# Smaller load pieces, a copy on another engine, and one hand-written list of steps between attention and experts

## Chip, cores and metric

One core of one Trainium2 chip. The metric is the device time of the kernel in microseconds (us). The engines are named as the profile names them: PE (matmul), PEld (its weight load), DVE (VectorE), ACT (ScalarE), POOL (GpSimd) and SP, which here only issues transfers.

## What is computed

Attention of 8 batches and 8 heads over 576 positions, in two forms that are added, and then an expert layer on the result (8 experts, 4608 tokens, one expert per token):

```python
q_d = q.reshape(B, H, Sd, factor, D).mean(axis=3)      # factor 4, Sd 144, k_d and v_d alike
out_up = np.repeat(sm_attn(q_d, k_d, v_d), factor, axis=2)
mask = np.abs(pos[:, None] - pos[None, :]) < factor     # local form: 7 neighbours
scores = np.where(mask, scale * np.matmul(q, k.transpose(0, 1, 3, 2)), -1000000000.0)
attn = np.exp(scores - np.max(scores, axis=-1, keepdims=True))
out_local = np.matmul(attn / (np.sum(attn, -1, keepdims=True) + 1e-09), v)
x = (out_up + out_local)                                # as 4608 rows of 512
...
logits = x @ w_gate
expert_idx = np.argmax(logits, axis=1)
gate_w = probs[np.arange(N), expert_idx]                # softmax of the logits
h = np.maximum(x_sorted[lo:hi] @ w1[e], 0.0)            # tokens of expert e
y_sorted[lo:hi] = h @ w2[e]                             # F = 1024
return gate_w[:, None] * y
```

## The kernel before, in words

The attention part is a software pipeline of 32 passes, one for each pair of heads. A table `PASS` lists pairs of a step and a lag; `steps(i)` walks it and calls each step for pass `i - lag`. The order of the table is the order in which each engine gets its instructions. Steps that the text speaks of:

- `load_qk` (L119) and `load_vd` (L207) load a pair's queries and keys (tile qk, one row per partition, queries then keys) and the values that are to be pooled (tile vd, 72 partitions); `load_vw` (L211) loads the local form's values. All are issued by SP, and each waits there until its buffer is free.
- `pool_qk` (L219, L225; tiles qkt, qkd) and `pool_v` (L230, L236; tiles vdt, vds) sum four neighbours on POOL in two steps each.
- `s_loc` (L245 adds the mask, L251 the scores; bank pS) on PE, then on DVE the maximum mx (L264), a subtraction (L268), after the exponential on ACT (L271) the sums (L274), the reciprocals and the scaling (L290); PE turns the result (L329). `s_d` (L305) has the pooled form's scores, `max_d` (L310, L313) their maximum. `add_up` (L385) adds both forms into the tile XT.
- Routing of a batch's rows (`r_mm` to `r_ix`, once per 4 or 5 tiles of 128 tokens) gives each token a row number. `x_rows` (L523, L525) turns a tile's tokens and evicts them into a row buffer xr, and `scatter` (L549, L550) writes them to the expert's rows in device memory (xs) by an indirect transfer, issued by POOL.

The expert part reads rows back with `x_load` (L586, issued by SP), turns them on DVE and splits them in two parts (`prep`: L617, ACT L621, DVE L622), multiplies by W1 (`s1`: L674 to L676, evicted by ACT L678 and DVE L679) and by W2 (`s2`: L688 to L690). The first 256 rows of expert 0 (`EARLY`) are read and multiplied before the last batch is routed, as those rows are surely full by then; `prep(0, 0, 1)` and the eight `s1(0, f, EARLY)` stand between the last passes. Rows 256 to 511 are read once the last scatter is done.

Where the passes end, the program before issues whole groups: `steps(31)`, then the first `x_load`, then `steps(32)`, the routing of the last batch's first four tiles, and so on (the end of the function below). Warm-up matmuls on zeros (`warm`, L138) stand ahead of pass 0 and behind passes 0, 1 and 2. The running count of tokens per expert, crun, gets its start value by a copy on DVE behind pass 2 (L925).

Of the kernel before, what the change touches and what calls it, by code (L numbers as in the profile page):

```python
# [29 lines left out]
KPAD = (NG - 1) * QB + KW  # L30
R = 4
# [12 lines left out]
WARM = (9, 5, 8, 5)  # L44
# [46 lines left out]
def attention_moe_kernel(ctx: ExitStack, tc: tile.TileContext, qk, vw, vd, wg, w1, w2, cst, csb, out):  # L91
# [33 lines left out]
    nc.scalar.dma_start(maskb, csb[:, B_MASK:])  # L125
# [9 lines left out]
    def warm(n, late=False):  # L135
        p = bank() if late else wp
        for _ in range(n):
            nc.tensor.matmul(p, wsrc[:, :128], wsrc, start=True, stop=True)  # L138
# [100 lines left out]
    def s_loc(i):  # L239
# [8 lines left out]
        for c in range(NC):  # L248
            for h, t in ((0, 0), (1, 1), (0, 1), (1, 0)):
# [3 lines left out]
                                 x[r, QPAD + g * QB:QPAD + g * QB + KW],  # L253
# [142 lines left out]
    def r_mm(m, tiles):  # L396
        c = tiles[0] * 128
        p = RS[m, "p"] = bank()
# [10 lines left out]
    def r_lg(m, tiles):  # L409
        lg = RS[m, "lg"] = rp.tile([128, 384], F32, name="over", bufs=1)  # L410
        w = 256 if len(tiles) == 4 else 384
        nc.scalar.activation(lg[:, :w], RS[m, "p"][:, :w], AF.Copy)

    def r_turn(m, tiles):
        lg = RS[m, "lg"]
        p = RS[m, "p"] = bank()
# [6 lines left out]
    def r_max(m, tiles):  # L423
        T = len(tiles)
        RS[m, "pl"] = RS[m, "p"][:, :T * 32].rearrange("p (t e) -> p t e", e=32)[:, :, :E]
        RS[m, "m"] = rp.tile([128, 5], F32, name="rm")
        nc.vector.tensor_reduce(RS[m, "m"][:, :T], RS[m, "pl"], axis=AX.X, op=OP.max)

    def r_sub(m, tiles):
        T = len(tiles)  # L430
        d = RS[m, "d"] = RS[m, "p"][:, 256:296].rearrange("p (t e) -> p t e", e=E)
        nc.vector.tensor_sub(d[:, :T], RS[m, "pl"], RS[m, "m"][:, :T, None].to_broadcast([128, T, E]))

    def r_exp(m, tiles):
        T = len(tiles)
        ex = RS[m, "ex"] = rp.tile([128, 5, E], F32, name="re")
        nc.scalar.activation(ex[:, :T], RS[m, "d"][:, :T], AF.Exp)

    def r_top(m, tiles):
        T = len(tiles)  # L440
        sc = RS[m, "sc"] = RS[m, "p"][:, 320:360].rearrange("p (t e) -> p t e", e=E)
# [632 lines left out]
```

## Time and profile before

| | us |
|---|---|
| three runs, median (lowest to highest) | 647.17 (645.33 to 647.36) |
| the profiled execution, its own time | 644.67 |
| its span in the profile | 642.9 |
| PE busy, share of the span | 96% |
| DVE, ACT, POOL busy | 55%, 53%, 35% |

The profile is of one execution. Times in rows count from the start of its span, and 1.8 us of the execution lie around that. The attention passes fill about the first 175 us, the passage into the experts ends near 225 us, and the experts take the rest.

### The profile page before, as it was taken

The numbers are of one execution on the slowest core, as the hardware profiler recorded it, in microseconds if no ns is written. First come the engines' busy times: TensorE is split into PE (matmuls) and PEld (weight loads), VectorE is DVE, ScalarE is ACT, GpSimd is POOL, SyncE is SP. The second block draws the span as 40 slices with busy tenths as digits, with TensorE's granted clock in tenths as the row PEclk, the third lists the DMA queues.
The fourth block names the chain that finished last, engine by engine and source line by source line (L and its number), as shares of the span: only waits on it lengthen the run. The fifth ranks groups of instructions, "written<-read, shape, count | busy, mean of one in ns | idle before, by whom it ended". The sixth has DMA issues, their size and how long they took to land.

```text
span 642.9 us, 15721 instructions
## 1 busy us (share of the span) xinstructions
PE 617.6 (96%) x6123; PEld 507.9 (79%) x6123; DVE 352.3 (55%) x691; ACT 343.3 (53%) x941; POOL 226.6 (35%) x348
## 2 busy tenths in 40 slices
PE   7899999999979899999999999999999999999994
PEld 4678887787768798888888888888888888888873
DVE  5999988888854573751571174175038166115020
ACT  4899999999964353543452263264235154223120
POOL 7877899999924311111111101101011111110111
PEclk9999999999989999999999999999999999999997
DMA  8998999999862794383274276258137537010001
GB/s 286 286 269 285 292 302 286 292 280 290 239 195 84 187 304 136 122 224 90 84 191 138 66 187 192 68 155 213 56 109 183 181 112 197 35 47 1 34 18 43
DMA packets 68612, 108.65 MB, mean 169 GB/s; under 512 B 15724, under 2 KB 39804, under 8 KB 68496
## 3 DMA queue, kind: packets, MB, share of 16 engines
q1 hardware_dynamic: 62080, 87.78, 49.0%
q0 software_dynamic: 5984, 19.01, 7.9%
q8 instruction: 66, 1.08, 0.8%
q14 instruction: 50, 0.41, 0.2%
q10 hardware_dynamic: 432, 0.37, 0.2%
HBM read 87.09 MB, written 23.67 MB: 172 GB/s over the span
## 4 chain that ended last, share of the span: by engine, by line
PE 68%; issue 10%; POOL 7%; DMA 5%; DVE 5%; ACT 2%; SPq 1%; POOLq 0%; another core or an unknown queue 0%; DVEq 0%; ACTq 0%
PE p L675 8%; PE p L674 8%; PE p L676 8%; PE p L690 7%; PE p L688 7%; PE p L689 7%; POOL xs L550 2%; DMA vd<-in_vd_dram 2%; PE pD L305 2%; POOL vdt L230 2%; PE pX L770 2%; PE pX L789 2%; PE pX L342 1%; PE pS L251 1%; PE pX L329 1%
## 5 line engine op out<-in xcount | busy, mean ns | idle before, releaser
L695 POOL DMA_INDIRECT out_dram<-y,tix x39 | 37.9, 971 | 213.3 <-ACT y L707 201.9
L674 PE MATMUL p<-xh,w1h 128*128 128x512 f32 (+1 forms) x288 | 106.4, 370 | 0.8 <-ACT xh L621 0.7
L675 PE MATMUL p<-xl,w1h 128*128 128x512 f32 (+1 forms) x288 | 105.7, 367 | 0.8 <-DVE xl L622 0.8
L676 PE MATMUL p<-xh,w1l 128*128 128x512 f32 (+1 forms) x288 | 105.5, 366 | 0.0
L688 PE MATMUL p<-w2h,hh 128*128 128x512 f32 x256 | 101.1, 395 | 0.0
L689 PE MATMUL p<-w2l,hh 128*128 128x512 f32 x256 | 99.8, 390 | 0.5 <-DVE w2l L664 0.5
L690 PE MATMUL p<-w2h,hl 128*128 128x512 f32 x256 | 99.9, 390 | 0.0
L679 DVE SCALAR_TENSOR_TENSOR hl<-p,hh 128x512 fp32r<-128x512 f32 (+1 forms) x72 | 45.5, 632 | 94.3 <-ACT hh L678 93.6
L678 ACT ACTIVATE hh<-p 128x512 fp32r<-128x512 f32 (+1 forms) x72 | 39.6, 551 | 78.1 <-PE p L676 75.6
L707 ACT ACTIVATE y<-p,gi 128x512 f32<-128x512 f32 x32 | 22.0, 689 | 91.2 <-PE p L690 86.8
L674 PEld LDWEIGHTS p<-xh,w1h 128*128 128x128 f32 x288 | 54.7, 190 | 10.7 <-ACT xh L621 1.1
L675 PEld LDWEIGHTS p<-xl,w1h 128*128 128x128 f32 x288 | 54.7, 190 | 9.6 <-DVE xl L622 0.9
L676 PEld LDWEIGHTS p<-xh,w1l 128*128 128x128 f32 x288 | 54.6, 190 | 8.7
L689 PEld LDWEIGHTS p<-w2l,hh 128*128 128x128 f32 x256 | 48.1, 188 | 10.6 <-DVE w2l L664 0.9
L690 PEld LDWEIGHTS p<-w2h,hl 128*128 128x128 f32 x256 | 48.1, 188 | 10.2
L688 PEld LDWEIGHTS p<-w2h,hh 128*128 128x128 f32 x256 | 48.1, 188 | 9.5
L664 DVE TENSOR_TENSOR w2l<-raw,w2h 128x512 fp32r<-128x512 f32 x64 | 43.3, 681 | 2.1 <-DMA xs<-xr,ix 1.5
L622 DVE TENSOR_TENSOR xl<-pX,xh 128x512 fp32r<-128x512 f32 x38 | 24.7, 684 | 35.2 <-ACT xh L621 34.2
L194 ACT ACTIVATE w1h<-raw 128x512 fp32r<-128x512 f32 (+1 forms) x72 | 42.1, 584 | 0.0
L550 POOL DMA_INDIRECT xs<-xr,ix x36 | 36.4, 1012 | 15.6 <-ACT xr L525 6.9
L663 ACT ACTIVATE w2h<-raw 128x512 fp32r<-128x512 f32 x64 | 39.8, 626 | 2.8 <-DMA xs<-xr,ix 2.8
L230 POOL TENSOR_TENSOR vdt<-vd 72x512 f32<-72x512 f32 x32 | 40.9, 1279 | 0.3
(152 smaller groups left out, 1240.1 us busy)
## 6 DMA issues: line engine op xcount, KB each, us to landing
raw<-in_w_dram SPq DMA_DIRECT2D x59, 512.0 KB
qk<-in_qk_dram SPq DMA_DIRECT2D x32, 583.0 KB
vw<-in_vw_dram SPq DMA_DIRECT2D x32, 320.0 KB
vd<-in_vd_dram SPq DMA_DIRECT2D x32, 288.0 KB
xrow<-xs SPq DMA_DIRECT2D x32, 192.0 KB
xrow<-xs SPq DMA_DIRECT2D x32, 128.0 KB
xs<-zs SPq DMA_DIRECT2D x6, 512.0 KB
raw<-in_w_dram SPq DMA_DIRECT2D x20, 128.0 KB
```

What stands on the lines that cost most here:

```text
L194: nc.scalar.activation(hi[:, s], src[:, s], AF.Copy)
L230: nc.gpsimd.tensor_add(t2, v[:, 0:2], v[:, 2:4])
L550: ins = nc.gpsimd.indirect_dma_start(out=xs, out_offset=bass.IndirectOffsetOnAxis(ap=IDX[m, t], axis=0), in_=xr, in_offset=None)
L663: nc.scalar.activation(hi, src, AF.Copy)
L664: nc.vector.tensor_sub(lo, src, hi)
L674: nc.tensor.matmul(p, wh[:, fs], xh[:, k, r], start=(k == 0), stop=False)
L675: nc.tensor.matmul(p, wh[:, fs], xl[:, k, r], start=False, stop=False)
L676: nc.tensor.matmul(p, wl[:, fs], xh[:, k, r], start=False, stop=(k == 3))
L679: nc.vector.scalar_tensor_tensor(hl[:, f, r], p, 0.0, hh[:, f, r], op0=OP.max, op1=OP.subtract)
L688: nc.tensor.matmul(p, hh, wh, start=(f == 0), stop=False)
L689: nc.tensor.matmul(p, hh, wl, start=False, stop=False)
L690: nc.tensor.matmul(p, hl, wh, start=False, stop=(f == 7))
```

## The change

It has six parts.

1. The tile qk gets two halves of 586 elements, each with a pad of 2 (the queries' half is filled up to the keys' length), and its load writes the halves as two pieces per partition. The tile vd gets four rows of 256 with a pad of 2, and its load four pieces per partition. The reads on POOL and PE use the new strides.
2. The mask is loaded by SP, between the first two loads of qk; before, by ACT.
3. The copy into crun runs on ACT.
4. The warm-up: 4 matmuls behind pass 0; in passes 2 and 3 a step `keep`, right behind `s_loc`, with 7 and 5.
5. `early_count` comes one pass sooner.
6. The last pass, what is left of the others, the last batch's routing and the early part of expert 0 become one list of single steps, `TAIL`. Steps that were one function (turn and evict rows; matmul, evict and subtract of an expert block; the two halves of a split weight) are single entries of it.

```diff
+KOFF = KPAD + 2
-WARM = (9, 5, 8, 5)
+WARM = (9, 4, 7, 5)
...
-        QK[i] = p1.tile([128, QPAD + KPAD], F32, name="qk", bufs=3)
-        nc.sync.dma_start(QK[i], qk[i])
+        QK[i] = p1.tile([128, 2 * KOFF], F32, name="qk", bufs=3)
+        nc.sync.dma_start(QK[i].rearrange("p (a x) -> p a x", a=2)[:, :, :KPAD], qk[i].rearrange("p (a x) -> p a x", a=2))
...
-    nc.scalar.dma_start(maskb, csb[:, B_MASK:])
+    nc.sync.dma_start(maskb, csb[:, B_MASK:])
...
-        VD[i] = p1.tile([DC, R, 2, 2, D], F32, name="vd")
-        nc.sync.dma_start(VD[i].rearrange("p r c h d -> p (r c h d)"), vd[i])
+        VD[i] = p1.tile([DC, R, 4 * D + 2], F32, name="vd")
+        nc.sync.dma_start(VD[i][:, :, :4 * D], vd[i].rearrange("p (r x) -> p r x", r=R))
...
-            return bass.AP(tensor=x.tensor, offset=x.offset + r, ap=[x.ap[0], [QPAD + HALO, 2], [R, SD], [2, 2]])
+            return bass.AP(tensor=x.tensor, offset=x.offset + r, ap=[x.ap[0], [KOFF + HALO, 2], [R, SD], [2, 2]])
...
-        v = VD[i]
+        v = VD[i][:, :, :4 * D].rearrange("p r (c h d) -> p r c h d", c=2, h=2)
...
+    def keep(i):
+        if 2 <= i < len(WARM):
+            warm(WARM[i])
+
     PASS = (
-        (exp_loc, 1), (rb_turn, 5), (t_d0, 3), (rc_place, 6), (eps, 2), (max_d, 1), (inv, 2), (s_loc, 0),
+        (exp_loc, 1), (rb_turn, 5), (t_d0, 3), (rc_place, 6), (eps, 2), (max_d, 1), (inv, 2), (s_loc, 0), (keep, 0),
...
+    TAIL = (
+        (exp_loc, 30), (s_loc, 31), (max_d, 30), (pool_v2, 30), (r_mm, 3, FIRST4), (eps, 29), (inv_d, 29),
...
+        (r_lg, 3, FIRST4), (sums, 30), (scatter, 2, 6), (e_d0, 28), (s_d, 31), (sub_loc, 31), (pool_v, 31),
+        (pool_v2, 31), (r_turn, 3, FIRST4), (r_max, 3, FIRST4), (x_tr, 2, 7), (x_ev, 2, 8), (norm_d, 29),
+        (r_sub, 3, FIRST4), (eps, 30), (scatter, 2, 8), (x_ev, 2, 7), (shut,), (t_d1, 29), (x_in,), (max_d, 31),
...
+        (r_cs, 3, FIRST4), (x_tr, 3, 1), (ld_vw, 30), (s1_mm, 7), (sums, 31), (x_ev, 3, 3), (r_eps, 3, FIRST4),
+        (ld_vw, 31), (add_up, 29), (eps, 31), (s1_mm, 4), (t_d1, 30), (x_ev, 3, 2), (s1_hi, 7), (x_ev, 3, 1),
...
+        (out_d, 30), (s1_lo, 7), (t_d0, 31), (e_d0, 31), (w2_in,), (t_d1, 31), (e_d1, 31), (r_last, 3, FIRST4),
+        (w2_hi, 0), (s1_mm, 5), (s1_hi, 4), (add_up, 30), (pv_d, 31), (pv_loc, 31), (scatter, 2, 7), (w2_hi, 1),
+        (out_d, 31), (w2_hi, 3), (w2_hi, 2), (scatter, 3, 3), (s1_lo, 4), (add_up, 31), (scatter, 3, 2), (w2_lo, 1),
...
+        (r_run, 3, LAST5), (w2_lo, 5), (scatter, 3, 6), (scatter, 3, 5), (totals,), (s1_lo, 2), (s1_mm, 0),
+        (s1_hi, 0), (s1_mm, 1), (s1_hi, 1), (scatter, 3, 8), (s1_lo, 0), (scatter, 3, 4), (scatter, 3, 7), (s1_lo, 1),
+    )
...
-    for i in range(NP):
+    for i in range(NP - 1):
         steps(i)
-        if i + 1 < len(WARM):
-            warm(WARM[i + 1], i >= 3)
+        if i == 0:
+            warm(WARM[1])
         if i == 2:
-            nc.vector.tensor_copy(crun, cf[:, C_CAP:C_CAP + E])
+            nc.scalar.copy(crun, cf[:, C_CAP:C_CAP + E])
...
-    steps(NP)
-    route_b(m, first)
...
-    totals()
+    for f, *a in TAIL:
+        f(*a)
```

`x_in` of the list is the first `x_load`, with the tiles that its rows are split into.

On DVE the copy into crun stood behind the sums of pass 2 and ahead of the pooled form's maximum. This is the place in the difference of DVE's instructions:

```order
 L268 TENSOR_TENSOR A<-pS,mx 128x2x5x64
 L274 TENSOR_REDUCE smd<-A 128x10
-L925 COPY crun<-cf 128x8
 L310 TENSOR_REDUCE mxd<-pD 128x3
 L282 RECIPROCAL pD<-smd 128x10
```

It is gone from there. The same place in the difference of ACT's instructions, where A is the scores' tile and AT the turned one:

```order
 L336 ACTIVATE AT<-pX 128x232
 L336 ACTIVATE AT<-pX 128x348
+L1032 COPY crun<-cf 128x8
 L271 ACTIVATE A<-A 128x640
 L277 ACTIVATE smd<-smd 128x13
```

The copy now stands ahead of the next pass's exponential.

POOL at the last pass, before: the scatter of tile 6 of batch 2, the last pair's value sums, the scatters of tiles 7 and 8, and the row numbers read back for expert 0:

```order
L550 DMA xs_83<-xr_126,ix_4003 42112x514
L230 TENSOR_TENSOR vdt_4296<-vd_4082 72x512
L236 TENSOR_TENSOR vds_4370<-vdt_4296 72x256
L549 MEMSET spacer_116 1x1
L550 DMA xs_83<-xr_126,ix_4003 42112x514
L549 MEMSET spacer_116 1x1
L550 DMA xs_83<-xr_126,ix_4003 42112x514
L605 CAST tix_4524<-gi_4318 128x2
```

And now:

```order
L557 DMA xs_83<-xr_126,ix_4004 42112x514
L230 TENSOR_TENSOR vdt_4247<-vd_4080 72x512
L236 TENSOR_TENSOR vds_4249<-vdt_4247 72x256
L556 MEMSET spacer_116 1x1
L557 DMA xs_83<-xr_126,ix_4004 42112x514
L482 TENSOR_TENSOR crun_112<-crun_112,cs_4430 128x8
L497 CAST ix_4521<-pos_4519 128x4
L556 MEMSET spacer_116 1x1
L557 DMA xs_83<-xr_126,ix_4004 42112x514
```

The second scatter is now that of tile 8, and the third, that of tile 7, stands behind the count and the row numbers of the last batch's first four tiles. In the program the first `x_load` stood behind the first of these scatters and now stands behind the second.

SP at the same place, before: value loads of the last pairs (vw), the read-back of expert 0's first rows (xrow0) and its gates (gi), three loads of raw W2, and the last pair's values:

```order
L211 DMA vw_4271<-in_vw_dram 128x640
L586 DMA xrow0_4313<-xs_83 32x8x128 x4
L598 DMA gi_4318<-xs_83 128x2x2
L168 DMA raw_4320<-in_w2_dram 128x2x512
L168 DMA raw_4322<-in_w2_dram 128x2x512
L168 DMA raw_4324<-in_w2_dram 128x2x512
L211 DMA vw_4388<-in_vw_dram 128x640
```

And now:

```order
L593 DMA xrow0_4282<-xs_83 32x8x128 x4
L605 DMA gi_4383<-xs_83 128x2x2
L211 DMA vw_4437<-in_vw_dram 128x640
L211 DMA vw_4455<-in_vw_dram 128x640
L168 DMA raw_4536<-in_w2_dram 128x2x512
L168 DMA raw_4538<-in_w2_dram 128x2x512
L168 DMA raw_4540<-in_w2_dram 128x2x512
```

Both value loads now stand behind the read-back and ahead of the W2 loads.

## Rows read from the trace of the kernel before

**Rows 1.** The page: busy us, share of the span, instructions, by engine.
```profile
PE 617.6 (96%) x6123; PEld 507.9 (79%) x6123; DVE 352.3 (55%) x691; ACT 343.3 (53%) x941; POOL 226.6 (35%) x348
```

**Rows 2.** Windows: stretch, its length, busy us by engine, clock, DMA share, GB/s.
```profile
20.00:40.00 20.00, 18.42 (x472) 14.85 (x476) 19.45 (x38) 18.78 (x72) 15.19 (x18) 1.00 0.97 282
...
80.00:100.00 20.00, 19.78 (x488) 16.45 (x487) 17.46 (x44) 19.36 (x74) 19.24 (x27) 1.00 1.00 296
...
120.00:140.00 20.00, 19.40 (x481) 16.05 (x483) 16.26 (x38) 19.06 (x69) 19.24 (x26) 1.00 0.95 294
...
180.00:200.00 20.00, 15.71 (x200) 12.79 (x198) 9.35 (x30) 10.12 (x33) 3.76 (x10) 0.91 0.50 146
...
240.00:630.00 390.00, 389.57 (x1748) 321.86 (x1747) 163.06 (x263) 150.16 (x271) 49.46 (x95) 1.00 0.42 118
```

**Rows 3.** Timeline of the start: start, us, instruction, [idle before and its releaser].
```profile
5.72 0.33 PE L245 MATMUL pS<-mask,cb 64*64 64x320 bf16 x4 [0.95 <-DMA mask<-in_csb_dram]
...
14.09 0.76 PE L329 MATMUL pX<-cf,A 128*128 128x128 f32 x5
...
14.23 0.82 DVE L264 TENSOR_REDUCE mx<-pS 128x10 f32<-128x640 f32 x1 [0.44 <-PE pS L251]
...
16.53 1.26 POOL L230 TENSOR_TENSOR vdt<-vd 72x512 f32<-72x512 f32 x1
16.56 2.37 DVE L925 COPY crun<-cf 128x8 f32<-128x8 f32 x1
...
17.75 1.14 POOL L219 TENSOR_TENSOR qkt<-qk 128x576 f32<-128x576 f32 x1
...
18.84 0.59 DVE L310 TENSOR_REDUCE mxd<-pD 128x3 f32<-128x432 f32 x1
```

**Rows 4.** The chain that ended last, at the tail: start, us, what.
```profile
174.98 3.51 DMA xs<-xr,ix
...
183.97 0.74 DVE p L617
...
212.00 3.29 DMA xs<-xr,ix
...
222.08 1.91 DVE pX L617 x3
```

**Rows 5.** Timeline of ACT, a small copy from the constants.
```profile
197.23 0.19 ACT L505 COPY xr<-cf 128x4 f32<-128x4 f32 x1
```

**Rows 6.** Waits of POOL, 20 to 60 us: total, times, longest us.
```profile
POOL qkt L219 <- DMA qk<-in_qk_dram: 6.5, 5, 1.8
```

**Rows 7.** The page, DMA queues: packets, MB, share of 16 engines' span.
```profile
q1 hardware_dynamic: 62080, 87.78, 49.0%
q0 software_dynamic: 5984, 19.01, 7.9%
...
q10 hardware_dynamic: 432, 0.37, 0.2%
```

**Rows 8.** POOL's groups by shape: busy us, mean ns | idle before.
```profile
L230 POOL TENSOR_TENSOR vdt<-vd 72x512 f32<-72x512 f32 x32 | 40.9, 1279 | 0.3
...
L236 POOL TENSOR_TENSOR vds<-vdt 72x256 f32<-72x256 f32 x32 | 23.2, 725 | 0.2
```

**Rows 9.** Timeline of POOL at the tail.
```profile
178.03 0.09 POOL L549 MEMSET spacer<- 1x1 f32 x1
184.82 0.98 POOL L550 DMA_INDIRECT xs<-xr,ix  x1 [6.71 <-ACT xr L525]
...
206.02 1.36 POOL L550 DMA_INDIRECT xs<-xr,ix  x1 [2.06 <-issue]
```

**Rows 10.** Timeline of DVE at the tail, the last sum of attention outputs.
```profile
195.05 0.83 DVE L385 TENSOR_TENSOR XT<-pPV,outd 128x290 f32<-128x290 f32 x2 [1.53 <-ACT outd L374]
```

**Rows 11.** Timeline of PE in expert 0's block: steps 1 and 14 of equal matmuls.
```profile
225.44 0.28 PE L676 MATMUL p<-xh,w1l 128*128 128x256 f32 x1
...
226.98 0.28 PE L674 MATMUL p<-xh,w1h 128*128 128x256 f32 x1
```

More of the change, by code (lines that the diff above doesn't have):

```diff
@@ L133, in attention_moe_kernel, with warm @@
     wp = psPV.tile([128, 1024], F32, name="pPV")[:, :512]
[L135 to L136 removed]
+    def warm(n):
         for _ in range(n):
[L138 removed]
+            nc.tensor.matmul(wp, wsrc[:, :128], wsrc, start=True, stop=True)
     warm(WARM[0])
@@ L656, in split_w2, with w2_open @@
     def split_w2(e, f):
-        if (e, f) == (0, 0):
-            home("tgi", 2)
-            home("ttix", 1)
-            home("gap", 16)
-        hi, lo = W2[e, f] = tuple(mp[f // 6].tile([128, DM], F32R, name=f"w2{n}{f}") for n in "hl")
-        src = raws[place[2, e, f // 2]][:, (f % 2) * 512:(f % 2) * 512 + 512]
-        nc.scalar.activation(hi, src, AF.Copy)
-        nc.vector.tensor_sub(lo, src, hi)
+        w2_open(e, f)
+        w2_part(e, f, 0)
+        w2_part(e, f, 1)
+    def w2_open(e, f):
+        W2[e, f] = tuple(mp[f // 6].tile([128, DM], F32R, name=f"w2{n}{f}") for n in "hl")
@@ L666, in s1, with w2_part, s1_part @@
+    def w2_part(e, f, n):
+        hi, lo = W2[e, f]
+        src = raws[place[2, e, f // 2]][:, (f % 2) * 512:(f % 2) * 512 + 512]
+        if n == 0:
+            nc.scalar.activation(hi, src, AF.Copy)
+        else:
+            nc.vector.tensor_sub(lo, src, hi)
+    HP = {}
     def s1(e, f, r=slice(0, FIRST)):
+        for n in range(3):
+            s1_part(e, f, r, n)
+    def s1_part(e, f, r, n):
         if e not in HT:
             HT[e] = tuple(mp[0].tile([128, 8, FIRST], F32R, name=f"h{w}") for w in "hl")
-        xh, xl = XH[e, 0]
@@ new lines, in s1_part @@
+        if n == 0:
+            xh, xl = XH[e, 0]
+            p = HP[e, f] = h_bank()[:, :r.stop - r.start]
+            fs = slice(f * 128, (f + 1) * 128)
+            for k in range(4):
+                wh, wl = W1[e, k]
+                nc.tensor.matmul(p, wh[:, fs], xh[:, k, r], start=(k == 0), stop=False)
+                nc.tensor.matmul(p, wh[:, fs], xl[:, k, r], start=False, stop=False)
+                nc.tensor.matmul(p, wl[:, fs], xh[:, k, r], start=False, stop=(k == 3))
+        elif n == 1:
+            nc.scalar.activation(hh[:, f, r], HP[e, f], AF.Relu)
+        else:
+            nc.vector.scalar_tensor_tensor(hl[:, f, r], HP.pop((e, f)), 0.0, hh[:, f, r], op0=OP.max, op1=OP.subtract)
@@ L916, in steps, with shut, x_in, gi_in @@
                 f(i - lag)
+    XP = {}
+    def shut():
+        close_p1.close()
+        close_s.close()
+        _, mp[0] = pool(name="m1", bufs=1)
+        _, mp["p1"] = pool(name="psM1", bufs=2, space=PSUM)
+    def x_in():
+        x_load(0, 0)
+        XH[0, 0] = tuple(mp[0].tile([128, 4, FIRST], F32R, name=f"x{w}0") for w in "hl")
+        HT[0] = tuple(mp[0].tile([128, 8, FIRST], F32R, name=f"h{w}") for w in "hl")
+    def gi_in():
+        gi_load(0, 0, 2)
+    def w2_in():
+        raw_ahead(8)
@@ new lines, in gi_out, with x_up, x_hi, x_lo @@
+    def gi_out():
+        gi_make(0, 0, 2)
+        home("tgi", 2)
+        home("ttix", 1)
+        home("gap", 16)
+    def x_up(t):
+        XP[t] = x_turn(XR[0, 0][:, t * 4:t * 4 + 4], h_bank)
+    def x_hi(t):
+        nc.scalar.activation(XH[0, 0][0][:, :, chunk(t)[1]], XP[t], AF.Copy)
+    def x_lo(t):
+        s = chunk(t)[1]
+        nc.vector.tensor_sub(XH[0, 0][1][:, :, s], XP.pop(t), XH[0, 0][0][:, :, s])
+    def s1_mm(f):
+        s1_part(0, f, EARLY, 0)
+    def s1_hi(f):
+        s1_part(0, f, EARLY, 1)
@@ L938, in attention_moe_kernel @@
-    m = B // 2 - 1
-    first, rest = list(range(4)), list(range(4, 9))
-    steps(NP)
-    route_b(m, first)
-    x_rows(m, 2)
-    x_rows(m, 3)
-    prep(0, 0, 1, get=h_bank)
-    steps(NP + 1)
-    s1(0, 0, EARLY)
-    gi_make(0, 0, 2)
-    steps(NP + 2)
-    steps(NP + 3)
-    route_a(m, rest)
-    route_c(m, first)
-    for t in (2, 3, 0, 1):
-        scatter(m, t)
-    route_b(m, rest)
-    x_rows(m, 6)
-    x_rows(m, 7)
-    s1(0, 1, EARLY)
-    route_c(m, rest)
-    x_rows(m, 8)
-    s1(0, 2, EARLY)
@@ L962, in attention_moe_kernel @@
-    x_rows(m, 4)
-    split_w2(0, 0)
-    s1(0, 3, EARLY)
-    x_rows(m, 5)
-    for f in (4, 5, 6, 7):
-        s1(0, f, EARLY)
-        if f == 4:
-            for t in rest:
-                scatter(m, t)
-        for j in (2 * f - 7, 2 * f - 6):
-            if j < 6:
-                split_w2(0, j)
-    totals()
+    for f, *a in TAIL:
+        f(*a)
     close_pv.close()
```

118 lines of the change are left out of this document (64 added, 54 removed).

## The prediction

> **What bounds the kernel now.** The page comes first: PE is busy 96% of the span [rows 1]. That is an average over two unlike halves, so the windows come next. In the expert part PE works 389.57 of 390 us at the full granted clock of 1.00 [rows 2]; nothing of the change lies there, so it can gain or lose only in the first 225 us. In the attention passes no engine stands out: from 20 to 40 us VectorE is fullest (19.45 of 20 us) with the DMA engines at a share of 0.97, in the windows from 80 and from 120 us ScalarE and POOL are (19.06 to 19.36) with the DMA at 1.00 and 0.95. From 180 to 200 us, where the passes end and the first expert begins, PE falls to 15.71 us and its mean clock to 0.91 [rows 2].
>
> Third comes the timeline of the first 24 us, as a delay there is passed on to all that follows. Two things to see: PE's first scores start after 0.95 us of waiting for the mask, and VectorE holds a copy of 8 numbers per partition (the count's start value) for 2.37 us [rows 3]. Fourth comes the chain that ended last, for the tail: it runs from a scatter of token rows at 174.98 us over the read-back to VectorE's transposes at 183.97, and again from the last scatter at 212.00 to the transposes at 222.08, behind which PE has the expert's own rows [rows 4].
>
> The profiled execution took 644.67 us with a span of 642.9; the median of the runs is 647.17, 2.5 us more. The sum is a difference, made against 644.67 and then applied to the median. What a measurement of this kernel can tell from no change is about 0.3%, 1.9 us.
>
> **Start: -3.3 us.** (1) The mask goes from ScalarE's queue to SP's, between the first two head-pair loads. PE's wait for it is 0.95 us [rows 3]. The mask can't come before the load ahead of it, so the whole wait is the upper bound and nothing the lower; I take two thirds, -0.6. VectorE waits for these scores, so the gain is handed on. The queue behind it on SP is the second pair's load, which now stands behind 160 KB more.
> (2) The warm-up of pass 1 moves behind the next scores, where 8 warm matmuls stood ahead of them; VectorE's wait for these scores at 14.23 is 0.44 us [rows 3]. It goes: -0.44. The warm matmuls then delay only transposes for which nobody is early; if they do delay them, the 0.44 comes back.
> (3) The copy. VectorE starts it at 16.56 and its next instruction at 18.84 [rows 3]: 2.28 us. On ScalarE the nearest row, a copy of 4 numbers from the same constant tile, takes 0.19 [rows 5], and ScalarE has 1.2 us free in the window from 20 us [rows 2]. Behind the copy on VectorE stand the maximum of the pooled scores and the whole pass, and VectorE is then the fullest engine, so I take all of it: -2.28. What did the copy wait for? It started 0.03 us after POOL's sum vdt began and ended (18.93) 0.04 us after POOL's next sum qkt ended (18.89); the constants were there, since PE used the same tile at 14.09 [rows 3]. The Trainium skill, page "SBUF — State Buffer", section "SBUF: two separate sides", says that VectorE and GpSimd share a port pair as an exclusive lock, which an fp32 copy within SBUF can need and which ScalarE does not use. The trace agrees: the copy spans two POOL sums; by that rule the 2.28 us go entirely.
> Together -0.6 - 0.44 - 2.28 = -3.3; with the whole of the mask's wait -3.7. The lower end is -1.0: POOL waited 6.5 us in 5 passes for head-pair loads [rows 6], so if those loads come no sooner, most of the shift ends as waiting there.
>
> **Loads: +0.6 us.** Each head-pair load is cut from 128 pieces of 4664 bytes to 256 of 2344, each pooled-value load from 72 of 4096 to 288 of 1024: 128 + 216 = 344 packets more per pass, with bytes nearly unchanged. The trace has no such row; the price of a packet comes from the queues. A packet of q1 (1414 bytes) took 0.490 x 16 x 642.9 / 62080 = 81 ns, one of q0 (3177 bytes) 136 ns, one of q10 (857 bytes) about 48 ns [rows 7]. A line through q0 and q1 leaves 37 ns that do not depend on bytes, one through q1 and q10 none; between them I take 15 ns. Then 344 x 15 / 16 engines = 0.32 us of DMA time per pass. Where transfers are hidden that costs nothing; the cover is the work of VectorE, ScalarE and POOL, and it is thin, with the DMA at 0.95 to 1.00 [rows 2]. POOL waited for a load in only 5 passes, all before 60 us [rows 6], and there VectorE is fuller, so I count two of them: 2 x 0.32 = +0.6.
> The Trainium skill, page "DMA: Bandwidth & Descriptors", section "Why small descriptors are slow (HBM only)", speaks against the change: a fixed overhead of some 3 cycles and 32 bytes of metadata per packet. An estimate by that page is 5 ns per packet, 0.1 us per pass, 3.2 us for 32 passes if none is hidden; no run here shows it yet.
> The rows of the pooled values get a pad, so POOL's first sum reads with other strides. It took 1279 ns for 512 columns, where the second took 725 for 256 [rows 8]. By columns the first could reach 2 x 725 = 1450 or fall to about 1000; POOL is nearly full from 80 to 160 us if the windows between are like the two shown, and at 175 us for 32 passes (5.5 us each) that is some 16 passes, so the two ends are +2.7 and -4.1. The sum keeps its operands' sizes: I take no change. Bounds of the loads with the packets: -4.1 (POOL alone) and +5.7 (the third rival); the likeliest case keeps -1.0 to +2.3.
>
> **Tail: +0.5 us.** The read-back of expert 0's first rows waits for the scatter before it in the program. That was the one at 174.98, and VectorE had the rows at 183.97, 9.0 us later [rows 4]. In the new list it stands behind two scatters. POOL reaches the second behind two sums, at the spacer of 178.03 [rows 9], issues at about 178.3, and the rows come at 178.3 + 9.0 = 187.3: 3.3 us later. (What POOL did next before, wait until 184.82 for a free row [rows 9], goes.) Between rows and the last sum of attention outputs (195.05 plus 0.83 [rows 10]: 11.9 us after the rows) the new list has two more blocks of 12 expert matmuls on PE; 13 steps took 226.98 - 225.44 = 1.54 us [rows 11], so 1.4 us per block, less some cover: +2.5. From there to the end of the last scatter it was 212.97 - 195.88 = 17.1 us; the two blocks are no longer in it, and POOL's wait of 2.06 us ahead of the scatter at 206.02 [rows 9] goes, since the scatters now follow their evictions: -2.8 - 2.06, of which 3.6 is counted, as the other engines' steps there stay. The last scatter comes +3.3 + 2.5 - 3.6 = +2.2 us, and behind it hangs the second read-back. That is the upper bound. If POOL issues that early scatter as soon as the row is evicted, some 3.3 us sooner, it is -1.1. Between them I take the middle, +0.5. The three W2 loads now come behind two value loads on SP; PE has expert blocks to hide that.
>
> **Sum:** -3.3 + 0.6 + 0.5 = -2.2; own time 642.5, on the median 645.0 us.
>
> **The rivals.** (A) *The loads help.* POOL's sum on padded rows falls to 1.02 us, worth about -4 where POOL is back to back, or the smaller pieces let scatters and read-backs through, and the tail takes its lower bound: about 641. For it: POOL's 19.24 of 20 us [rows 2]. Against it: the sum's size is the same, and ScalarE stands as full beside it.
> (B) *The start's gain is taken back by loads.* The DMA engines are at 0.97 from 20 us on; 3.3 us gained ahead of them become waits of POOL for head-pair loads, as the 6.5 us there are already [rows 6]: 0 + 0.6 + 0.5 = +1.1, 648.3. Here too belongs that the copy does not do what is thought: were it waiting for its data, ScalarE would wait as long and hold up the exponentials; the use of that tile at 14.09 speaks against it.
> (C) *The other side: the DMA engines become the bound of every pass.* With a share of 0.95 to 1.00 the 18 passes (5.5 us each) between 60 and 160 us pay 0.32 us each: +5.7, in all -3.3 + 5.7 + 0.5 = +2.9, 650.0. It decides from (3.3 - 0.5) / 18 = 0.16 us per pass on. For it: the share [rows 2]. Against it: no wait of POOL for a load after 60 us [rows 6].
>
> **How the numbers follow.** My case 0.48, (A) 0.16, (B) 0.17, (C) 0.19. The predicted time is 645.0; its own range is 643 to 647.5 from the bounds of the mask, the loads and the tail. It lies near the line of 0.3% (645.2): three fifths of my case are faster, the rest the same. Faster: 0.29 + 0.16 = about 0.46. Same: 0.19 + most of (B), 0.12, = 0.31. Slower: (C) and the rest of (B), 0.23. The range of 8 in 10 reaches into (A) and to (C): 640.5 to 650.
>
> **What the profile would show.** Start: no copy on VectorE, the step to the pooled maximum without a gap at 16 us, and every later pass some 3 us earlier. If passes at 60 us stand where they did, (B). Loads: POOL's mean for vdt near 1279 ns, a wait of POOL for qk after 60 us in case of (C), a lower mean in case of (A). Tail: VectorE's transposes of the first rows some 12 us before the last attention sum, and PE's first block behind the second read-back half a microsecond later than the passes' end would give. The forecast is wrong if the passes' own period changes by more than 0.16 us, since 28 of them stand behind the start and my sum has no such term.

## The result, and the profile after

| | before | changed |
|---|---|---|
| median of the runs, us (lowest to highest) | 647.26 (645.33 to 648.45) | 655.07 (653.54 to 659.51) |
| profiled execution, its span, us | 644.67, 642.9 | 653.54, 651.8 |
| ratio to before, 95% interval | | 1.0137 (1.0095 to 1.0179) |

The changed kernel is slower by 1.4%, where 645.0 us, a gain, was forecast; the range ended at 650.0. The two profiled executions are 8.9 us apart. VectorE's maximum of a pass's scores (line 264, once per pass) serves as a mile stone:

| | before | changed | apart |
|---|---|---|---|
| maximum of pass 3, us | 20.5 | 18.8 | -1.7 |
| of pass 8 | 44.8 | 48.3 | +3.5 |
| of pass 31, the last | 172.9 | 179.6 | +6.7 |
| last scatter issued | 212.0 | 220.5 | +8.5 |
| end of the span | 642.9 | 651.8 | +8.9 |

So in this pair of profiles the start gained 1.7 us, 28 passes lost 8.4 us (0.30 us each), the tail lost 1.8 us, and the experts 0.4. A pair shows where two executions differ and not yet what the change costs: the same program's passes take longer in some executions than in others, as the section "Both kernels once more" shows. First the page of the changed kernel, busy time and queues, to be read against [rows 1, 7]:

```profile
PE 619.9 (95%) x6118; PEld 509.5 (78%) x6121; DVE 349.3 (54%) x690; ACT 344.2 (53%) x942; POOL 226.4 (35%) x348
...
q1 hardware_dynamic: 73232, 88.05, 49.7%
q0 software_dynamic: 5984, 19.01, 7.8%
q8 instruction: 66, 1.08, 0.7%
```

No engine has much more work. Queue q1 carries 11,152 packets more (144 of them the mask's, which left q10) with nearly the same bytes, and was busy 0.497 x 16 x 651.8 = 5183 us of engine time against 5040: 143 us more, 13 ns per added packet. The windows, as in [rows 2]:

```profile
20.00:40.00 20.00, 17.86 (x411) 14.20 (x411) 15.75 (x31) 15.35 (x57) 14.95 (x17) 0.91 1.02 274
80.00:100.00 20.00, 18.36 (x463) 15.16 (x459) 15.58 (x36) 17.53 (x64) 18.12 (x25) 1.00 0.95 289
120.00:140.00 20.00, 19.41 (x484) 16.05 (x483) 17.16 (x41) 19.37 (x71) 19.44 (x26) 1.00 0.96 284
180.00:200.00 20.00, 13.79 (x173) 11.89 (x172) 11.26 (x29) 10.73 (x36) 5.58 (x11) 0.83 0.56 176
```

From 20 to 40 us VectorE fell from 19.45 to 15.75 us and ScalarE from 18.78 to 15.35, with the DMA share up from 0.97 to 1.02 at fewer bytes: these engines now wait, and the window has 0.91 of the clock. A part of that comes and goes by itself: in a second profile of the kernel before (before_again, below) they have 17.91 and 17.35 us there. At the start (timeline, as in [rows 3]) the copy is gone from VectorE:

```profile
5.79 0.33 PE L245 MATMUL pS<-mask,cb 64*64 64x320 bf16 x4 [0.67 <-DMA mask<-in_csb_dram]
...
16.49 0.21 ACT L1032 COPY crun<-cf 128x8 f32<-128x8 f32 x1
...
16.18 0.81 DVE L274 TENSOR_REDUCE smd<-A 128x10 f32<-128x640 f32 x1
17.10 0.61 DVE L310 TENSOR_REDUCE mxd<-pD 128x3 f32<-128x432 f32 x1
...
18.81 0.82 DVE L264 TENSOR_REDUCE mx<-pS 128x10 f32<-128x640 f32 x1
```

The copy cost ScalarE 0.21 us, and the step of VectorE behind the sums came 0.1 us after them. PE's first scores start at 5.79, though, not sooner than 5.72, and still wait for the mask. Then the waits (total, times, longest us), POOL's from 20 to 60 us and PE's from 20 to 175:

```profile
POOL qkt L219 <- DMA qk<-in_qk_dram: 9.5, 6, 2.0
...
PE pPV L357 <- issue: 4.6, 6, 1.4
PE pS L251 <- issue: 2.8, 2, 2.1
```

POOL's wait of [rows 6] has grown from 6.5 to 9.5 us. The two lines of PE were 0.6 and 1.6 us before. "Issue" means that no semaphore explains the wait. Where it stands in PE's timeline, with two windows of it:

```profile
28.03 0.72 PE L251 MATMUL pS<-qk 64*58 64x64 f32 x37
30.89 0.32 PE L251 MATMUL pS<-qk 64*58 64x64 f32 x3 [2.14 <-issue]
...
33.80 1.71 PE L305 MATMUL pD<-qkd 64*64 64x144 f32 x12
```

```profile
30.00:32.00 2.00, 1.11 (x47) 1.05 (x48) 0.75 (x1) 0.84 (x6) 0.74 (x1) 1.00 1.00 285
32.00:34.00 2.00, 2.00 (x15) 1.33 (x13) 1.97 (x5) 0.87 (x3) 2.00 (x4) 0.55 1.01 289
```

PE stopped for 2.14 us within a group of 40 equal matmuls, 37 of them done, and no semaphore explains it. The granted clock then fell to 0.55, near the lower level of 1.2 GHz, and the pooled scores took 1.71 us where they take 0.95. What it waited for can be read from the trace's record of DMA packets of kind "instruction" (queue q8 has 66 of 16,384 bytes, which are taken here for PE's program). All stops of over 0.5 us within a group up to 175 us, with the packet that ended last ahead of each:

```
matmul no.   PE resumes   stood, us   packet ended   resumes after
   472         30.89        2.14         29.28            1.61
   725         42.45        0.60         40.97            1.48
  1483         75.69        0.74         74.22            1.47
  1609         82.33        1.44         80.84            1.49
  3254        155.90        1.27        154.44            1.46
  3635        173.59        0.66        171.97            1.62
```

They stand 253, 758, 126, 1645 and 381 matmuls apart, multiples of 126.5, and end 1.5 to 1.6 us after the end of such a packet. Stops stand at the same matmuls in other profiles, with big pieces too: no. 472 in before_again, e1, e4 and e9, no. 1609 in e1, e4 and e9. That fits a PE that has used up its code and waits for the next packet; 126.5 matmuls with as many weight loads would have 65 bytes each of a packet. No run shows it by itself. The profile counts q8's packets into the time of the 16 DMA engines, as it does those of the loads. The Trainium skill, page "Runtime: NRT & Kernel Launch", section "Terms", has the instruction memory as a FIFO that is refilled in 16 KiB blocks; the trace agrees, with 1.08 MB in 66 packets.

The tail: VectorE's and POOL's timeline, two windows, and the chain that ended last:

```profile
184.27 0.98 POOL L557 DMA_INDIRECT xs<-xr,ix  x1 [0.15 <-ACT ADT L350]
```

```profile
192.77 1.32 DVE L624 STREAM_TRANSPOSE p<-xrow 128x512 f32<-128x512 f32 x2 [5.83 <-DMA xrow<-xs]
```

```profile
188.00:192.00 4.00, 1.39 (x14) 0.95 (x14) 0.00 (x0) 0.22 (x2) 0.00 (x0) 1.00 0.67 141
192.00:196.00 4.00, 1.77 (x9) 1.78 (x10) 3.10 (x7) 2.42 (x9) 0.04 (x1) 0.58 1.01 302
196.00:200.00 4.00, 4.00 (x22) 4.00 (x22) 2.43 (x7) 2.16 (x10) 0.77 (x4) 0.57 0.66 252
```

```profile
220.47 3.42 DMA xs<-xr,ix
225.64 4.95 DMA xrow<-xs
230.71 1.91 DVE pX L624 x3
```

The rows of expert 0 came 8.5 us after the scatter of tile 8. In [rows 4, 9] the same rows came 9.0 us after a scatter that POOL issued one turn earlier. The stretch from 5 to 13 us after the last maximum, in the kernel before and then in the changed one, and four microseconds of the kernel before:

```profile
177.87:185.87 8.00, 6.02 (x117) 4.57 (x115) 5.35 (x16) 6.33 (x23) 1.29 (x4) 1.00 0.68 139
```

```profile
184.61:192.61 8.00, 4.39 (x108) 3.26 (x106) 1.68 (x5) 2.81 (x10) 0.64 (x1) 1.00 0.48 110
```

```profile
188.00:192.00 4.00, 3.90 (x21) 3.90 (x22) 0.83 (x2) 1.93 (x5) 0.00 (x0) 0.57 0.67 257
```

PE, which had 6.02 us of work there, now has 4.39. Behind that wait the clock is low in both kernels, but longer in the changed one: 0.57 from 188 to 192 us before, 0.57 to 0.58 from 192 to 200 us now.

### The profile page after: what moved, and what is told of

Same layout as the page of the kernel before. It is cut to its first block, busy times and chain, and to the rows that moved or that the text cites. A ratio compares the mean times of both kernels' runs of the same rounds, so it can differ in the third digit from the quotient of the medians.

```text
span 651.8 us, 15709 instructions
## 1 busy us (share of the span) xinstructions
PE 619.9 (95%) x6118; PEld 509.5 (78%) x6121; DVE 349.3 (54%) x690; ACT 344.2 (53%) x942; POOL 226.4 (35%) x348
## 3 DMA queue, kind: packets, MB, share of 16 engines
q8 instruction: 66, 1.08, 0.7%
## 4 chain that ended last, share of the span: by engine, by line
PE 77%; issue 10%; DMA 5%; POOL 3%; ACT 2%; DVE 1%; SPq 1%; POOLq 0%; another core or an unknown queue 0%; DVEq 0%
PE p L695 9%; PE p L696 9%; PE p L697 8%; PE p L712 7%; PE p L711 7%; PE p L710 7%; PE pD L305 3%; PE pX L342 3%; PE pPV L357 3%; PE pX L329 2%; PE pPV L370 2%; PE pS L251 2%; PE pX L523 2%; PE pX L792 2%; PE pX L811 2%
## 5 line engine op out<-in xcount | busy, mean ns | idle before, releaser
L717 POOL DMA_INDIRECT out_dram<-y,tix x39 | 37.9, 971 | 212.9 <-ACT y L729 201.5
L219 POOL TENSOR_TENSOR qkt<-qk 128x576 f32<-128x576 f32 x32 | 36.7, 1146 | 16.6 <-DMA qk<-in_qk_dram 16.4
L230 POOL TENSOR_TENSOR vdt<-vd 72x512 f32<-72x512 f32 x32 | 41.0, 1280 | 0.2
```

## The experiments

Each was timed in turn with the kernel before on one chip; ratios are to that. Executions spread more in these sets than in the first runs (the medians of before were 647 to 653 us), so the intervals are about 0.3 to 0.6% to either side. The sets ran on three chips, so two ratios of different sets are compared with more caution than their intervals alone ask for. Times of stages come from one profiled execution each.

### The parts, one by one

**e1, big pieces in the changed kernel.**

```diff
-KOFF = KPAD + 2
+KOFF = KPAD
-        nc.sync.dma_start(QK[i].rearrange("p (a x) -> p a x", a=2)[:, :, :KPAD], ...
+        nc.sync.dma_start(QK[i], qk[i])
-        VD[i] = p1.tile([DC, R, 4 * D + 2], F32, name="vd")
+        VD[i] = p1.tile([DC, R, 4 * D], F32, name="vd")
```

Expected: 

> The changed kernel with the loads in big pieces again (head-pair tile one piece of 4688 bytes per partition, pooled values one of 4096); mask, copy, warm-up and list stay changed. Theory (the small pieces slow the loads, the first pass above all, and cost +8.4 us in the passes): 647.3 - 3.3 (start) + 1.9 (tail) = about 646, ratio 0.998 to the kernel before, and the maximum of the last pass stands at about 170 to 172 us instead of 179.6. Rival (the new place of the mask on SP and the later warm-up hold up the loads behind them): stays near 653 to 655, ratio 1.01.

Measured: 1.012 (1.006 to 1.018), last maximum at 180.4 us, last scatter 43.7 us later. The theory fell as the only cause: with big pieces most of the loss is still there, and the last maximum stands no earlier than the 179.6 us of the changed kernel. The rival did not show either, as e8 and e14 say below. The stretch of 43.7 us, against 37.9 to 39.1 in the kernel before, points to the tail (e13).

**e2, small pieces alone on the kernel before**, the reverse edit. Expected: 

> The kernel before with the small pieces alone. Theory: the passes alone lose 6 to 8 us, 654 us, ratio 1.010 to 1.013, and the loads of the first 16 us take 20% longer. Rival (mask and warm-up): within 1 us of the kernel before.

Measured: 1.006 (1.002 to 1.010); the last scatter 39.6 us after the last maximum, as before. The pieces cost, but 4 us, less than expected.

**e3, the copy alone**: `nc.scalar.copy(crun, ...)` for `nc.vector.tensor_copy(crun, ...)`. Expected: 

> The kernel before with the copy of the count on ScalarE alone. Theory (the copy's 2.3 us on VectorE is handed on to the end): 645.0, ratio 0.9965. Rival (the loads take the gain back in the passes that follow, as POOL already waits for them): 647 and ratio 1.000, with pass 3 two us earlier and pass 12 where it was.

Measured: 1.0007 (0.9973 to 1.0041). The rival's time holds: pass 3 stands at 19.3 us, pass 8 at 46.9, no gain. But nothing had to be taken back, as the copy is seldom long. On VectorE, in before_again and in e7:

```profile
18.27 1.25 DVE L925 COPY crun<-cf 128x8 f32<-128x8 f32 x1
```

```profile
18.17 0.16 DVE L1032 COPY crun<-cf 128x8 f32<-128x8 f32 x1
```

Eleven profiles, with the first of the kernel before, have the copy on VectorE. In ten of them it took 0.16 to 1.25 us, seven times under 0.5; the 2.37 us of [rows 3] is the longest. In all eleven it ended within 0.1 us after the end of a POOL sum, as if it waited for the sum that was running, and for two sums in the first profile.

**e4, the list alone** (big pieces, mask, copy, warm-up and `early_count` as before). Expected: 

> The kernel before with the list of single steps alone (loads, mask, copy, warm-up and early count as before). Theory (the first rows of expert 0 now wait for a later scatter): +1.9 us, 649.2, ratio 1.003, with PE idle for 5 us between the passes' end and the transposed rows. Rival (the list's order itself is as good, and what the tail lost in the changed kernel came from the late passes): 647, ratio 1.000.

Measured: 1.0054 (1.0019 to 1.0089), 43.6 us from the last maximum to the last scatter where the kernel before has 37.9 to 39.1. The theory's sign is there, a late read-back, and its 1.003 lies within the interval.

**e7, the list with one entry moved:**

```diff
-        ..., (scatter, 2, 8), (x_ev, 2, 7), (shut,), (t_d1, 29), (x_in,), (max_d, 31),
+        ..., (x_ev, 2, 7), (shut,), (t_d1, 29), (x_in,), (scatter, 2, 8), (max_d, 31),
```

Expected: 

> The list alone on the kernel before, with one entry moved: the read-back of expert 0's first rows ahead of the scatter of tile 8, as in the kernel before (there the scatter waits for it). Theory (what the list loses is that wait): the 5 us of idle PE before the transposed rows fall to 2, ratio 1.000 against 1.0054 of the list as it is. Rival (the rest of the list's order loses as much): ratio 1.004 to 1.006 as before.

Measured: 1.0048 (1.0011 to 1.0085), so by the time alone the rival holds: it can't be told from e4. The profile shows what the entry does in the tail: the rows are on VectorE at 189.75 us, 8.1 us after the scatter of tile 6 at 181.69, and the last scatter is 39.0 us after the last maximum. Its chain:

```profile
181.69 3.21 DMA xs<-xr,ix
186.30 1.80 DMA xrow<-xs
```

and the stretch from 5 to 13 us after the last maximum in windows, e7 first and then e4:

```profile
184.84:192.84 8.00, 5.99 (x121) 4.62 (x120) 4.64 (x12) 5.08 (x18) 0.98 (x2) 1.00 0.41 101
```

```profile
188.11:196.11 8.00, 4.54 (x108) 3.40 (x106) 1.67 (x5) 2.80 (x10) 0.45 (x1) 1.00 0.50 128
```

PE gets 1.45 us back in these 8 us, and VectorE 3.0, and behind them the clock does not fall in e7. So e7's tail is that of the kernel before, and its passes are the same program; where its 0.5% is lost stays open.

**e13, the changed kernel with big pieces and that entry moved.** Expected: 

> The changed kernel with two of its parts mended: big pieces in both loads, and the first read-back of the list ahead of the scatter of tile 8. Theory (the parts add: start 0 to 0.3%, list 0.2%): ratio 1.001 to 1.005, against 1.012 with big pieces alone. Rival (start and list make each other worse): 1.008 to 1.014.

Measured: 1.0031 (0.9994 to 1.0067), against 1.012 of e1, the same but for the entry; the last scatter 36.4 us after the last maximum. The times differ by 0.9% (0.2 to 1.6, from two sets on two chips), the stretches by 7.3 us. So the place of the first read-back costs several us in the changed kernel.

**e15, the changed kernel with only that entry moved.** Expected: 

> The changed kernel with one entry of the list moved: the first read-back ahead of the scatter of tile 8. Theory (the read-back behind the later scatter costs 4 to 6 us, as between e1 and e13, and the small pieces the rest): ratio 1.005 to 1.011, 43 us from the last pass's maximum to the last scatter falling to 38 to 40. Rival (the small pieces carry the whole loss, and the tail only waits for the same loads): 1.012 to 1.020.

Measured: 1.0094 (1.0060 to 1.0128), 38.5 us from the last maximum to the last scatter. The rest of the loss, some 6 us, stands with the small pieces and the start's edits; e13, which has those edits and big pieces, stands at +2, and its interval reaches to 0.

**e8, the three edits of the start alone** (mask, copy, warm-up). Expected: 

> The kernel before with the three edits of the start (mask on SP's queue, copy on ScalarE, later warm-up). Prediction as on record (-3.3 us): ratio 0.995. Theory now (the loads of the first passes take it back): 0.998 to 1.002. Rival (the mask ahead of the second pair's load puts off all loads behind it, as the difference between e1 and e4 would have it): 1.004 to 1.008.

Measured: 1.0031 (1.0002 to 1.0059), between the theory and the rival, and not the gain on record. Maxima of passes 3, 8 and 31 of e8, then of the kernel before on the same chip (before_again, below):

```profile
18.11 0.82 DVE L264 TENSOR_REDUCE mx<-pS 128x10 f32<-128x640 f32 x1
...
45.88 0.81 DVE L264 TENSOR_REDUCE mx<-pS 128x10 f32<-128x640 f32 x1
...
174.16 0.82 DVE L264 TENSOR_REDUCE mx<-pS 128x10 f32<-128x640 f32 x1
```

```profile
21.13 0.82 DVE L264 TENSOR_REDUCE mx<-pS 128x10 f32<-128x640 f32 x1
...
47.84 0.81 DVE L264 TENSOR_REDUCE mx<-pS 128x10 f32<-128x640 f32 x1
...
176.17 0.82 DVE L264 TENSOR_REDUCE mx<-pS 128x10 f32<-128x640 f32 x1
```

Of 3.0 us, 2.0 are left at pass 8, and still at pass 31. But this profile is of e8's fastest execution (644.45 us, where the median is 649.13), so it doesn't show how the median run loses its lead; the times show only that there is no gain.

**e14, the mask alone** (`nc.sync.dma_start(maskb, ...)`). Expected: 

> The kernel before with the mask's load on SP alone. Prediction's term (-0.6 us handed on): 0.999. Theory now (whatever the first passes gain, later loads take back): 0.998 to 1.002. Rival (it is the mask that makes the start's three edits slower by 0.3%, as the second pair's load stands behind it): 1.002 to 1.006.

Measured: 0.9984 (0.9949 to 1.0018): no effect that shows, and not the rival.

**e16, mask and copy, warm-up as before.** Expected: 

> The kernel before with the two start edits that cost nothing alone, the mask on SP's queue and the copy on ScalarE, with the warm-up as before: the version that could beat both kernels. Prediction's terms (-0.6 and -2.3 us, handed on): 0.9955. Theory now (later loads take it back): 0.998 to 1.001, and the later warm-up is then what makes the three edits of e8 slower. Rival (the three edits of e8 were slower by chance): 1.002 to 1.005.

Measured: 1.0023 (0.9988 to 1.0058). Neither the forecast gain nor proof that the warm-up costs; no version with the right values was faster beyond its interval than the kernel before.

### What a small piece costs

**e9, still more pieces**: the head-pair load as in the change, the pooled values in eight pieces of 512 bytes.

```diff
+        VD[i] = p1.tile([DC, R, 2, 2 * D + 2], F32, name="vd")
+        nc.sync.dma_start(VD[i][:, :, :, :2 * D], vd[i].rearrange("p (r c x) -> p r c x", r=R, c=2))
```

Expected: 

> The kernel before with still smaller pieces: the head-pair load in two pieces per partition as in the change, the pooled values in eight of 512 bytes in place of four, so 632 more packets per pass than before in place of 344. Theory (each piece costs DMA time): the loss of the small pieces alone, 0.6%, grows by 632/344 to 1.1%, ratio 1.008 to 1.014. Rival (pads, strides or the new halves cost, whatever the number of pieces): 1.004 to 1.007.

Measured: 1.0126 (1.0081 to 1.0171); the loss grows with the number of pieces, and the rival's 1.004 to 1.007, pads and strides alone, lies outside the interval. POOL's first sum kept its time, 1284 ns. The page's queue, POOL's and PE's waits from 20 to 175 us, and two windows:

```profile
q1 hardware_dynamic: 82304, 87.88, 51.2%
```

```profile
POOL qkt L220 <- DMA qk<-in_qk_dram: 19.6, 15, 2.3
...
PE pPV L358 <- issue: 8.4, 11, 2.1
PE pS L252 <- issue: 4.9, 4, 1.8
```

```profile
20.00:40.00 20.00, 17.79 (x406) 13.97 (x394) 17.19 (x32) 16.66 (x63) 14.13 (x16) 0.91 1.03 263
80.00:100.00 20.00, 16.46 (x378) 13.10 (x377) 13.96 (x33) 16.40 (x58) 16.13 (x23) 1.00 1.01 262
```

20,224 packets more than before took 0.512 x 16 x 655.9 - 5040 = 333 us of engine time, 16 ns each. The bytes per second fall from 296 to 262 GB/s at a share that stays at 1.

**e11 and e12, one load at a time.** Expected for the head-pair load: 

> The kernel before with the head-pair load alone in two pieces per partition (128 more packets per pass). Theory (each packet costs, late loads and late code for PE follow): 128/344 of the loss of both, +0.2%, ratio 1.001 to 1.004; POOL's waits for qk between 20 and 175 us at 8 to 11 us. Rival (the head-pair load is the one that POOL waits for, so its pieces carry the whole loss): 1.005 to 1.009.

Expected for the pooled values: 

> The kernel before with the pooled-value load alone in four pieces per partition (216 more packets per pass, all on the engines that carry 72 partitions). Theory: 216/344 of the loss, +0.4%, ratio 1.003 to 1.007. Rival (the head-pair load carries the loss): 0.999 to 1.002.

Measured: 0.9994 (0.9962 to 1.0027) and 1.0026 (0.9996 to 1.0056). The order fits the number of packets (128 and 216) and speaks against the rival that the head-pair load carries the loss; but both are below the theory, neither loss shows by itself, and together they are 0.2%, where e2, with both, lost 0.6%.

**e5 and e6, fewer bytes**: every second load of the local values is left out, in the kernel before and in the changed one.

```diff
+        if i % 2 and i < 30:
+            VW[i] = VW[i - 1]
+            return
```

Expected: 

> The kernel before, in which every second load of the local form's values (passes 1 to 29) is left out and the pair before's values are used again, so that part of the result is another; 13% fewer bytes per pass. Theory (in the passes the DMA engines set the pace, through late loads and through late packets of PE's own code): no stall inside a group of matmuls over 0.3 us, no wait of POOL for a load after 30 us, 6 to 10 us less, ratio 0.985 to 0.991. Rival (PE, ScalarE and POOL set the pace, the loads only happen to be as full): ratio 0.998 to 1.002.

> The changed kernel with the same loads left out. Theory (the small pieces cost only through full DMA engines): the passes end within 1 us of the kernel before with the same loads left out, and the rest is the tail: 1.5 to 3 us above that one, ratio to the kernel before 0.988 to 0.995. Rival (small pieces cost by themselves, by their issue on SP or the strides that POOL and PE read): still 6 us or more above it.

Measured: 0.9916 (0.9882 to 0.9951) and 1.0007 (0.9968 to 1.0045). The first figure misleads: other values mean another routing, and from the last scatter to the last matmul e5 takes 413.7 us where all with the true values take 421 to 423, which is more than the 6.1 us by which its median is lower. The passes must be read alone. From pass 3 to pass 31 e5 takes 157.9 us, e7 on the same chip with all loads 158.8, and e6 166.1. So 13% fewer bytes in the passes' three loads, a DMA share of 0.84 in place of 0.90 up to 180 us, bring no gain that shows: the theory fell that the bytes set the pace. PE's stops remain in e5 (6.3 us). And e6 is 7.7 us above e5 by the medians, though its experts take less (411.9 us), and 8 us by the passes: the rival of e6 holds, small pieces cost with fewer bytes too.

**e10, the pooled values in two loads**, of 64 and 8 partitions. Expected: 

> The kernel before with each pooled-value load as two loads, of 64 and of 8 partitions, so that the pieces spread more evenly over the DMA engines, at one more issue on SP per pass. Theory (full DMA engines set the pace of the passes): 1 to 4 us less, ratio 0.994 to 0.999. Rival (the mean share is what counts, or the issue costs more): 1.000 to 1.004.

Measured: 1.0040 (1.0015 to 1.0066). The theory fell: with one more load per pass there is a loss and no gain. Its profile (644.98 us, 154.8 from pass 3 to pass 31) does not show where.

### Both kernels once more

Expected of the changed kernel: 

> The changed kernel once more, beside the others of this set on one chip. If its loss belongs to the kernel: ratio 1.010 to 1.018 here too. If a good part of it was the luck of late code for PE in the executions timed first (7.2 us of stalls inside groups of equal matmuls, against 2.1 in the profiled execution before): ratio 1.004 to 1.010, and the stalls in the profile move with the time.

Measured: 1.0224 (1.0169 to 1.0280), more than the first time; last maximum at 185.7 us. The loss is the kernel's, and its size is not the same in each set.

Expected of the kernel before, one profile: 

> The kernel before, unchanged, for a profile beside those of the experiments. Theory (the passes are paced by loads and by PE's code coming through the same DMA engines, and that differs from execution to execution): the maximum of the last pass stands some us later than the 172.9 of the first profile when the time is above 645, and stalls inside groups of equal matmuls add up to more than 3.7 us; the stretch from that maximum to the last scatter stays 39 us and the rest 421 us. Rival: the tail or the experts differ.

Measured: 648.19 us, last maximum at 176.2 us, 37.9 us to the last scatter, 422.8 on to the last matmul. The passes differ, nothing else. Side by side, from the profiles (us; waits from 20 to 175 us, PE's within groups):

| | pieces | POOL for qk | PE | last maximum |
|---|---|---|---|---|
| before, first profile | big | 6.5 | 2.2 | 172.9 |
| e8 | big | 8.8 | 4.1 | 174.2 |
| before_again | big | 8.7 | 5.0 | 176.2 |
| e7 | big | 6.5 | 4.7 | 179.8 |
| e1 | big | 7.2 | 8.2 | 180.4 |
| e3 | big | 11.1 | 7.2 | 181.2 |
| e4 | big | 9.0 | 8.8 | 183.1 |
| changed, first profile | small | 11.6 | 7.4 | 179.6 |
| e2 | small | 10.0 | 8.1 | 185.2 |
| after_again | small | 14.3 | 9.1 | 185.7 |
| e9 | smallest | 19.6 | 13.3 | 187.0 |

Small pieces stand at the high end of both waits, but kernels with big pieces reach it too: e1, e3 and e4 have as long stops of PE as the changed kernel (in e1 and e4 a quarter to a third of the sum are stops of up to 0.5 us that do not stand 1.4 to 1.7 us behind a packet of code). So neither wait is the mark of small pieces. The first profile of the kernel before is the fastest of its kind in the passes. From pass 3 to pass 31, ten profiles with big pieces and all loads (e10 apart) take 152.3 to 163.6 us, mean 158.4; four with the pieces of the change (changed, after_again, e2, e15) take 160.8 to 166.8, mean 164.1. That is 5.7 us, 0.2 us per pass, in place of the 8.4 of the first pair. Queue q1 was busy for 4948 to 5102 us in the ten, for 5157 to 5231 in the four.

## Why the prediction was wrong

**Start, -3.3.** The step that failed is "VectorE starts it at 16.56 and its next instruction at 18.84 [rows 3]: 2.28 us", taken for the price of the copy. It was one execution's: in ten more profiles with the copy on VectorE it took 0.16 to 1.25 us, as it came early or late in a sum of POOL. The wait for POOL was read rightly, and the Trainium skill's rule of the shared port pair ("SBUF — State Buffer", "SBUF: two separate sides") agrees with it: 0.16 to 2.37 us on VectorE, each time up to the end of a POOL sum, 0.21 on ScalarE.

From pass 2 to pass 3 the changed kernel takes 4.22 us where the first profile took 6.30, but before_again took 5.18. Moving the copy alone left 4.73 (e3) or, with the mask, 5.15 (e16); with the later warm-up it is 4.23 (e8). So most of what the step gains on before_again goes with the warm-up, for which 0.44 was forecast. The mask's term of -0.6 was 0: on SP's queue the mask still ended PE's wait, at 5.79 us against 5.72. In all, pass 3 came at 18.1 to 19.7 us in seven profiles with the three edits and at 19.5 to 21.1 in eleven with the copy on VectorE, 1.5 us earlier in the mean. "So I take all of it" failed as well: the copy (e3) and the three edits (e8) gained nothing in the time. That is the outcome of rival (B), which had 0.17, but not by its mechanism as far as the runs show: POOL's waits for head-pair loads are 8.8 us in e8 and 8.7 in before_again.

**Loads, +0.6.** The step that failed is the cover, "I count two of them". The passes from 3 to 31 take 5.7 us longer by the means, 0.2 us each, and the timed runs of the pieces alone lost 3.9 us (e2, 0.6%). That every pass pays is what rival (C) said, which had 0.19; its reason, that the DMA engines become the bound of every pass, is not shown, and e5, where fewer bytes brought nothing, speaks against it in the kernel before. The price in DMA time was near: 15 ns per packet was taken, 13 and 16 measured. That 0.32 us per pass was forecast and 0.30 seen in the first pair is luck, since that pair has the fastest profile before. "No wait of POOL for a load after 60 us" [rows 6] was no evidence that loads are hidden: in the changed kernel POOL waits there for 2.1 us only. PE's stops within groups were not in the sum, and no list of waits by semaphore shows their reason; but they are as long in kernels with big pieces, so they tell executions apart more than the two kernels. The Trainium skill ("DMA: Bandwidth & Descriptors", "Why small descriptors are slow (HBM only)") spoke against the change, rightly. The estimate from it, 5 ns per packet, is a third of the DMA time measured; its 3.2 us for all passes are near the 3.9 us of e2. POOL's sum on padded rows kept its 1280 ns, as forecast.

**Tail, +0.5.** The forecast had the rows 3.3 us later against the passes' end; they came 13.2 us after the last maximum against 11.1, 2.1 later. From the last maximum to the last scatter it was 40.9 us against 39.1: +1.8, near the upper bound of +2.2 and not the middle, and 43.4 to 43.7 in three later profiles of the list (after_again, e1, e4), +4.5 and above that bound. With the one entry moved it is 36.4 to 39.0 (e7, e13, e15). The step that failed is "between them I take the middle": POOL did not issue that scatter early, it reached it as the walk said, behind two sums (184.27, 4.7 us after the last maximum; before that spacer stood 5.2 us after it). And the clock was left out: behind PE's wait for the rows it is low for some 8 us, where it was low for some 4 in the kernel before. It is not low there in e7, e13 and e15, with the entry moved. But other profiles with the old tail have a low clock there for as long (e2, e3, e9), or none (e14), so it is no mark of the list.

The parts add up to the loss: nothing gained at the start, 4 to 6 us for the pieces, 2 to 5 us for the place of the read-back, against 7.8 us between the medians. They can't be set apart more finely, since the times of different sets give 0.6% for the pieces alone (e2) and 0.2 to 1.0% between e1 and the two sets of the changed kernel; for the entry they give 0.9% (e1 against e13), 0.4 to 1.3% (e15 against those two sets) and nothing between e4 and e7. Shown are the number of pieces as a cause (e2, e9) and the entry of the list as the cause of the longer tail (the stage times of e1, e4, after_again against e7, e13, e15). Open is by what a piece costs. In DMA time q1 is busy for longer. SP's issue of a pooled-value load takes 0.80 us in place of 0.32 (medians); but it takes as long in e9, which has 632 packets more per pass where e2 has 344 and lost twice as much, which speaks against the issue as the whole of it. e10 had one more issue per pass without smaller bytes and lost 0.4%, so the issue is not cleared. Open too is why the same kernel lost 1.4% in one set and 2.2% in another.

## What to carry to other kernels

Count the packets, not only the bytes, when a load is cut up: with DMA engines near a share of 1 their time was paid in every pass here. Before a wait is put into a sum as a gain, look for it in a second profile: one that depends on where another engine stands can be 0.2 us in the next execution. Look for stops inside a group of equal matmuls: no semaphore explains them, and here most followed a packet of code. When steps are put into another order, find for each read-back the last write ahead of it in the program, as that one sets when it may start.

## What the runs showed that had not been expected

PE's code, as the stops would have it, is a load like any other: one packet of 16,384 bytes per 126.5 matmuls, about one per pass, that started, in the kernel before, 0.7 to 4.4 us after PE had gone over to the block before it (worked out from the trace by counting matmuls). With a packet of about 1.1 us and the 1.5 us behind it, at the upper end more than a whole pass (5.5 us) is used up, so that in the kernel before PE already stands at this edge. After a stop of about 2 us the granted clock was 0.55 to 0.60 for some 4 us. The same copy took between 0.16 and 2.37 us on VectorE, by where POOL stood. And a profile of this kernel holds for its execution: in a second one the unchanged kernel's last maximum came 3.3 us later, with PE's stops at 5.0 us in place of 2.2.
